# Rows of y by pure transposes, router logits by four column groups and a summing product: one change to a tuned attention-and-router kernel

## The chip, the cores and the metric

The kernel runs on one core of one Trainium2 chip. The metric is the device time in microseconds (us) of one execution of the whole program; the figure compared is the median over runs. Engines are named as the profile names them: PE is TensorE, PEld its weight loads, DVE VectorE, ACT ScalarE, POOL GpSimd, and SP the engine that issues most transfers.

## What the reference computes

A gated linear attention over 4 batches, 8 heads, 768 steps and 48 channels per head gives `y`. Its rows, seen as 3072 tokens of 384 channels, go through a router with two experts of eight per token. Cut to what matters here:

```python
for t in range(S):
    state = alpha[:, :, t, :, None] * state + np.einsum('bhd,bhe->bhde', k[:, :, t], v[:, :, t])
    y[:, :, t] = np.einsum('bhd,bhde->bhe', q[:, :, t], state)
x = np.ascontiguousarray(y.transpose(0, 2, 1, 3)).reshape(B * S, H * D)
logits = x @ w_gate
noise_scale = np.log1p(np.exp(x @ w_noise))
noisy_logits = logits + noise_scale * noise
top2 = np.argpartition(-noisy_logits, 2, axis=1)[:, :2]      # then a softmax over the two
h = np.maximum(x[mask] @ w1[e], 0.0)                          # for each expert e
out[mask] += top2_w[mask, k, None] * (h @ w2[e])
```

## The kernel before, in words

The tokens are cut into 24 **chunks** of 128 (six per batch). The attention runs chunk by chunk, with all eight heads as four pairs (`NP` = 4); a pair takes 128 partitions, 64 for each head, 48 of them used. The results of a chunk stand in `yT`, channels on partitions and tokens along the row.

The order of all work is written out by hand: every engine carries out its own queue in program order. The loop over `n` is one **chunk turn**. It emits pieces in the order of the string `ORDER`: among others `keys`, `alphas` and `queries` (four transposes each, L343, of the inputs of a later chunk), `turn_y` (rows of the chunk before, below), `turn_k` (four transposes of scaled keys, L450), `output` (products L491 and L252 into `y`, then the copy of `y` to `yT` on ACT, L494, or L487 in two halves at the start of a batch), `no_more` (an activation and the reading of its accumulator on ACT, L361), `state` (products L465), `scores` (products L423), `masked` (two masked copies on DVE, L443) and `products` (a scan on DVE, L371). `inverses` is the second scan on DVE, L383, to `over`. In the last chunk of a batch `state`, `turn_k` and `block` fall out of the turn that would prepare them, and in the first the product L491 does. A turn begins on PE with the eight transposes of `keys` and `alphas`.

`turn_y` is `rows_of`: for each pair one matrix product of `yT` with `to_rows` (L275), whose columns hold an identity that drops the unused channels, and beside it the router weights of the pair. One product so gives rows of y and a part of the logits, two pairs to a part. ACT copies the logits to `lgs` (L277), and the rows of y in two 16-bit planes to `y_sb` (L282), which SP writes to memory.

Routing of six chunks (`routing`, a generator) is cut into steps; `ROUTE` lists after which turn and place each step of the first two units comes (the turn is counted from the last chunk of the unit). The first steps are: the sum of the logits' parts on DVE (`lg`, L713) with an exponential on ACT (L719); a logarithm on ACT, ahead of which its table is loaded (L687); products with the noise (L728) and maxima on DVE; and then an exponential for the gates, again with a table load (L751). From turn 22 on, the pairs of expert tiles follow, ordered by due times in units of `T` = 20; `out_of_range` is one step among them.

Transfers, POOL's scaling of the keys (L401) and the PSUM pools (`h`: two buffers, used by `rows_of` and by products of the router) are unchanged in kind.

Of the kernel before, what the change touches and what calls it, by code (L numbers as in the profile page):

```python
# [12 lines left out]
U16 = mybir.dt.uint16  # L13
# [6 lines left out]
def kernel(  # L20
# [189 lines left out]
    to_rows = const.tile([C, NP, 2 * D + 2 * E], F32, name="to_rows")  # L210

    def place_ident():
        nc.gpsimd.memset(to_rows, 0.0)
        for i in range(2):
            for odd in range(2):
                nc.gpsimd.tensor_copy(
                    out=to_rows.rearrange("p (j o) c -> p j o c", o=2)[:, :, odd, ds(2 * E * odd + D * i, D)],
                    in_=ident[:, None, ds(DP * i, D)].to_broadcast([C, NP // 2, D]))

    def router_tile(on):  # L220
        w_r = on["one"].tile([C, NP, 2, E], F32, name="w_r")
        nc.gpsimd.memset(w_r, 0.0)
        return w_r

# [5 lines left out]
    def place_router(w_r):  # L230
        for odd in range(2):
            nc.gpsimd.tensor_copy(
                out=to_rows.rearrange("p (j o) c -> p j o c", o=2)[:, :, odd, ds((1 - odd) * 2 * D, 2 * E)],
                in_=w_r.rearrange("p (j o) w e -> p j o (w e)", o=2)[:, :, odd])

# [31 lines left out]
    def rows_of(n, yT, on):  # L267
# [24 lines left out]
    def fast_gla(on):  # L292
# [212 lines left out]

        ROUTE = (((1, 9), (2, 8), (2, 13), (3, 4), (3, 11), (4, 8), (4, 10), (5, 4), (5, 7)), ((1, 9), (1, 12), (2, 4), (2, 8), (2, 11), (3, 8), (3, 10), (4, 4), (4, 7), (4, 12)))
        routes = [routing(u, on) for u in range(NU)]
# [12 lines left out]
        def out_of_range(part):  # L520

            if part:
# [15 lines left out]
        return (load, load_v, alphas, no_more, products, inverses, keys, scaled_keys, queries, scores, masked, turn_k,  # L538
                state, block, output, turn_y, put_y, route, route_on, all_routed, out_of_range, places,
                clear_blocks, clear_yT)  # L540
# [559 lines left out]
    def pairs(on):  # L1100
# [11 lines left out]
        x_whole = x_turned.rearrange("p s w a t -> p s (w a t)").bitcast(F32)  # L1112
        xs = block([C, C], "xs", 5)
        hs = [block([C, FO // 2, C], f"h{f}", 2) for f in range(2)]
# [570 lines left out]
    with ExitStack() as es:  # L1685
        on = pools(es, "")
        shared = on["one"].tile([C, 2 * (NP * (C + 1) + 1) + 4 * NP * C], F32, name="shared")
        (load, load_v, alphas, no_more, products, inverses, keys, scaled_keys, queries, scores, masked, turn_k,
         state, block, output, turn_y, put_y, route, route_on, all_routed, out_of_range, places,
         clear_blocks, clear_yT) = fast_gla(on)  # L1690
# [4 lines left out]
        def beside():  # L1695

            at = (-0.95, 4.75, 3.66, 6.15, 6.9, 28.5)
            left = [(at[0], lambda: put_y(LAST - 2)), (at[1], lambda: output(LAST)), (at[2], lambda: turn_y(LAST - 1)),
                    (at[3], lambda: turn_y(LAST)), (at[4], lambda: put_y(LAST - 1)), (at[5], lambda: put_y(LAST)),
                    (5 * T + 17.4, lambda: out_of_range(0)), (5 * T + 18.7, lambda: out_of_range(1))]  # L1700
            r1, r2, r3 = (6.2, 12.2, 15.2)
# [21 lines left out]
        NOISE_AT = (3, 8, 13, 18)  # L1723
        FIRST_ORDER = "scores masked inverses keys router scaled turn_k queries alphas output products state turn_y"
        SECOND_ORDER = "keys turn_y inverses turn_k scaled queries no_more block output state alphas scores masked products"
        ORDER = "keys inverses alphas turn_y turn_k scaled queries block output no_more state scores masked products"

        LATE_ORDER = "keys inverses alphas turn_y turn_k scaled block output no_more state scores masked queries products"

# [12 lines left out]
        with tc.manual_schedule():  # L1742
# [3 lines left out]
            load(1, "kq")  # L1746
            place_ident()
            clear_blocks()
# [35 lines left out]
            for n in range(LAST):  # L1784
# [5 lines left out]
                          "state": lambda: state(n + 1), "scores": lambda: scores(n + 1),  # L1790
                          "masked": lambda: masked(n + 1)}
                names = (FIRST_ORDER if n == 0 else SECOND_ORDER if n == 1 else LATE_ORDER if n == LAST - 2 else ORDER).split()
                if n == 0:
                    pieces["router"] = lambda: place_router(held.pop(0))
# [73 lines left out]
```

## Time and profile before

| what | value |
|---|---|
| median of 3 runs | 629.37 us (628.87 to 629.84) |
| the profiled execution's own time | 634.14 us |
| its span on the core | 632.5 us |
| mean granted TensorE clock | 0.995 |
| busy PE, DVE, ACT, POOL | 613.7, 512.2, 330.4, 323.2 us |

The trace is of one execution, whose own time is 4.77 us above the median; what is worked out from it is a difference, to be laid on the median. Busy times are unions over the span. The chunk turns lie between about 20 and 153 us, the expert tiles behind.

### The profile page before, as it was taken

The numbers are of one execution on the slowest core, as the hardware profiler recorded it, in microseconds if no ns is written. First come the engines' busy times: TensorE is split into PE (matmuls) and PEld (weight loads), VectorE is DVE, ScalarE is ACT, GpSimd is POOL, SyncE is SP. The second block draws the span as 40 slices with busy tenths as digits, with TensorE's granted clock in tenths as the row PEclk, the third lists the DMA queues.
The fourth block names the chain that finished last, engine by engine and source line by source line (L and its number), as shares of the span: only waits on it lengthen the run. The fifth ranks groups of instructions, "written<-read, shape, count | busy, mean of one in ns | idle before, by whom it ended". The sixth has DMA issues, their size and how long they took to land.

```text
span 632.5 us, 14445 instructions
## 1 busy us (share of the span) xinstructions
PE 613.7 (97%) x5326; PEld 589.3 (93%) x5326; DVE 512.2 (81%) x1175; ACT 330.4 (52%) x664; POOL 323.2 (51%) x362
## 2 busy tenths in 40 slices
PE   8999999999999999999999999999999999999993
PEld 5899989988999999999999999999999999989893
DVE  8788998878759877578999999787987879878671
ACT  5778777675555453342555454545545545454340
POOL 7353277854051877775545465532655427443353
PEclk9999999999999999999999999999999999999997
DMA  9999999984862666785746776866869578775223
GB/s 144 167 199 214 219 201 170 226 160 112 264 194 100 205 199 182 205 248 98 176 103 134 176 242 135 225 149 154 260 161 234 123 181 226 178 213 134 63 40 53
DMA packets 178288, 108.56 MB, mean 172 GB/s; under 512 B 142600, under 2 KB 167667, under 8 KB 178209
## 3 DMA queue, kind: packets, MB, share of 16 engines
q1 hardware_dynamic: 137040, 33.59, 31.1%
q10 hardware_dynamic: 25840, 53.48, 27.7%
q0 software_dynamic: 15328, 20.47, 14.5%
q8 instruction: 44, 0.72, 0.5%
q14 instruction: 36, 0.29, 0.1%
HBM read 85.85 MB, written 24.22 MB: 174 GB/s over the span
## 4 chain that ended last, share of the span: by engine, by line
PE 75%; DVE 12%; issue 3%; DMA 3%; POOL 2%; ACT 2%; SPq 0%; POOLq 0%; DVEq 0%; ACTq 0%
PE h_ps L1338 14%; PE sc L1331 13%; PE o_ps L1338 11%; PE sc L1323 7%; PE c_ps L1331 6%; PE tp L343 5%; PE sc L423 4%; PE y L252 4%; PE h_ps L275 3%; PE y L491 3%; DVE wt L1204 1%; PE o_ps L465 1%; PE tp L450 1%; PE c_ps L1323 1%; DVE h L1207 1%
## 5 line engine op out<-in xcount | busy, mean ns | idle before, releaser
L972 POOL DMA_INDIRECT out_dram<-o,where x46 | 48.5, 1055 | 150.4 <-DVE o L1356 70.4
L1342 ACT ACTIVATE h<-h 128x512 f32<-128x512 f32 x89 | 55.2, 628 | 84.4 <-DVE h L1204 51.6
L988 POOL DMA_INDIRECT x_in<-x_rows,where x48 | 59.6, 1242 | 53.9 <-DVE where L1172 29.5
L980 POOL DMA_INDIRECT out_dram<-o,where x44 | 74.7, 1697 | 13.4 <-issue 13.4
L1338 PE MATMUL o_ps<-wt,hx 128*128 128x192 f32 x384 | 70.7, 327 | 0.0
L1338 PEld LDWEIGHTS o_ps<-wt,hx 128*128 128x128 f32 x384 | 61.5, 190 | 1.8 <-issue 1.8
L172 POOL DMA_INDIRECT table<-entry,place_u x48 | 53.1, 1106 | 13.9 <-issue 10.9
L1331 PE MATMUL sc<-yT,ws 128*128 128x128 f32 x408 | 56.5, 275 | 0.0
L1331 PEld LDWEIGHTS sc<-yT,ws 128*128 128x128 f32 x408 | 53.5, 191 | 0.0
L401 POOL TENSOR_TENSOR k_P<-k_P,over 128x512 f32<-128x512 f32 (+1 forms) x24 | 27.7, 1155 | 44.6 <-DVE over L383 31.5
L343 PE MATMUL tp<-ident,ins 128*128 128x128 f32 x288 | 42.0, 280 | 2.2 <-ACT k_P L393 0.7
L1352 ACT ACTIVATE o<-h_ps,tab 128x192 f32<-128x192 f32 x46 | 19.3, 420 | 40.9 <-PE h_ps L1338 33.7
L343 PEld LDWEIGHTS tp<-ident,ins 128*128 128x128 f32 x288 | 31.8, 142 | 7.2 <-ACT k_P L393 1.1
L443 DVE COPY_PREDICATED shared<-upto,sc 128x512 f32<-128x512 uint32 x47 | 31.9, 732 | 6.9 <-PE sc L423 6.4
L1338 PE MATMUL h_ps<-w,hx 128*128 128x192 f32 x192 | 35.6, 327 | 0.3 <-issue 0.3
L1338 PE MATMUL h_ps<-wt,h 128*128 128x192 f32 x192 | 35.3, 327 | 0.3 <-DVE wt L1204 0.3
L1338 PE MATMUL o_ps<-w,h 128*128 128x192 f32 x192 | 35.3, 327 | 0.2 <-DVE o L1360 0.2
L1338 PE MATMUL h_ps<-wt,hx 128*128 128x192 f32 x192 | 35.2, 326 | 0.0
L1338 PE MATMUL h_ps<-w,h 128*128 128x192 f32 x192 | 35.1, 326 | 0.0
L1198 ACT COPY xt<-x_turned 128x768 uint16<-128x768 uint16 x34 | 33.6, 1053 | 0.8 <-DMA x_turned<-x_in 0.8
L1338 PEld LDWEIGHTS h_ps<-w,hx 128*128 128x128 f32 x192 | 31.7, 190 | 0.7 <-issue 0.7
L1338 PEld LDWEIGHTS h_ps<-w,h 128*128 128x128 f32 x192 | 31.8, 190 | 0.0
(322 smaller groups left out, 1642.1 us busy)
## 6 DMA issues: line engine op xcount, KB each, us to landing
w<-in_moe_w_dram ACTq DMA_DIRECT2D x42, 512.0 KB
w<-in_moe_w_dram ACTq DMA_DIRECT2D x56, 384.0 KB
ins<-in_alpha_dram SPq DMA_DIRECT2D x24, 192.0 KB
ins<-in_k_dram SPq DMA_DIRECT2D x24, 192.0 KB
ins<-in_q_dram SPq DMA_DIRECT2D x24, 192.0 KB
vt<-in_v_dram SPq DMA_DIRECT2D x24, 192.0 KB
x_rows<-y_sb SPq DMA_DIRECT2D x24, 192.0 KB
ins<-in_moe_w_dram ACTq DMA_DIRECT2D x9, 512.0 KB
```

The lines of the kernel that those rows point to most:

```text
L172: put = nc.gpsimd.indirect_dma_start(out=table, out_offset=bass.IndirectOffsetOnAxis(ap=place, axis=0), in_=entry, in_offset=None, bounds_ ...
L343: nc.tensor.transpose(tp[:, j, :], src[:, 2 * j:2 * j + 2, :], ident)
L401: (nc.vector if n == NT - 1 else nc.gpsimd).tensor_tensor(c["k"][:, at], c["k"][:, at], over[:, at, 1:CB], op=ALU.mult)
L443: nc.vector.copy_predicated(MTs[n % 2][:, i], mask_upto, sc)
L972: put = nc.gpsimd.indirect_dma_start(out=out, out_offset=bass.IndirectOffsetOnAxis(ap=at, axis=0), in_=rows, in_offset=None, bounds_check= ...
L980: add = nc.gpsimd.indirect_dma_start(out=out, out_offset=bass.IndirectOffsetOnAxis(ap=at, axis=0), in_=rows, in_offset=None, bounds_check= ...
L988: nc.gpsimd.indirect_dma_start(out=rows, out_offset=None, in_=x_rows[0:units * UT, :], in_offset=bass.IndirectOffsetOnAxis(ap=at, axis=0), ...
L1198: nc.scalar.copy(halves[:, part], x_turned[:, :, part].rearrange("p s a t -> p s (a t)"))
L1323: nc.tensor.matmul(bank[name][:, f, :], W[:, ds(f * C, C)], X, start=new and f == 0, stop=True, skip_group_check=True)
L1331: nc.tensor.matmul(bank[name][:, 2 * h + f, :], W[h][:, ds(f * C, C)], X[h], start=new and not h and not f, stop=True, skip_group_check=True)
L1338: nc.tensor.matmul(bank[name], H[:, f, :], W[:, f, :], start=new and f == 0, stop=True, skip_group_check=True)
L1342: nc.scalar.activation(t, t if src is None else src, AF.Relu)
```

## The change

Rows of y are now made by four plain transposes of `yT` for chunks 0 to 21 (`turned_rows`); chunks 22 and 23 keep `rows_of`. The logits of those chunks are a separate piece, `logits`, behind `state`: four products with the router weights `w_r` (32 columns for each pair, 16 of them zero) as the stationary operand, one to each quarter of the output partitions; ACT copies the result to a spare tile `xs`. In the first piece of the next turn `sum_pairs` multiplies this copy with `two_parts` (ones that add two pairs), which turns it too, and ACT copies the 32 columns to `lgs`. The first routing steps come one turn later. `to_rows` is filled after turn 6 instead of at the start, and the second part of `out_of_range` is due later.

```diff
+    def turned_rows(n, yT, on):
+        bank = on["h"].tile([C, FO // 2, C], F32, name="h_ps")
+        for j in range(NP):
+            nc.tensor.transpose(bank[:, j, :], yT[:, j, :], ident)
+        y_sb = on["three"].tile([C, 2, NP, 2 * D], U16, name="y_sb")
+        planes = bank.rearrange("p j t -> p (j t)").bitcast(U16).rearrange("p (h c w) -> p w h c", h=H, w=2)
+        for w in range(2):
+            nc.scalar.copy(y_sb[:, w].rearrange("p j (i c) -> p (j i) c", i=2), planes[:, w, :, 0:D])
+        return y_sb
+
+    def logits_by_pair(yT, w_r, by_pair, on):
+        bank = on["h"].tile([C, FO // 2, C], F32, name="h_ps")
+        for j in range(NP):
+            nc.tensor.matmul(bank[ds(4 * E * j, 4 * E), 0, :], w_r[:, j].rearrange("p w e -> p (w e)"), yT[:, j, :], start=True, stop=True)
+        nc.scalar.copy(by_pair, bank[:, 0, :])
+        return bank, by_pair
+
+    def logits_by_token(n, bank, by_pair):
+        nc.tensor.matmul(bank[:, 1, 0:4 * E], by_pair, two_parts, start=True, stop=True)
+        nc.scalar.copy(lgs[(n // UC) % 2][:, n % UC].rearrange("p a c -> p (a c)"), bank[:, 1, 0:4 * E])
...
-                chunks[n]["y"] = rows_of(n, chunks[n]["yT"], on)
+                chunks[n]["y"] = (turned_rows if n < NT - 2 else rows_of)(n, chunks[n]["yT"], on)
...
-                    (5 * T + 17.4, lambda: out_of_range(0)), (5 * T + 18.7, lambda: out_of_range(1))]
+                    (5 * T + 17.4, lambda: out_of_range(0)), (6 * T + 7.0, lambda: out_of_range(1))]
...
-        ORDER = "keys inverses alphas turn_y turn_k scaled queries block output no_more state scores masked products"
+        ORDER = "keys inverses alphas turn_y turn_k scaled queries block output no_more state logits scores masked products"
...
-            place_ident()
...
-                pieces = [lambda: (load_v(n + 2), load(n + 5, "a" if n != 1 else ""), load(n + 4, "kq"), put_y(n - 2))] + \
+                pieces = [lambda: (load_v(n + 2), load(n + 5, "a" if n != 1 else ""), load(n + 4, "kq"), put_y(n - 2), sum_pairs(n - 2))] + \
...
+                if n == 6:
+                    last.append(lambda: (place_ident(), place_router(held[0])))
```

In `ROUTE` the first entries of the first unit go from `(1, 9), (2, 8)` to `(2, 6), (2, 8)`, and of the second from `(1, 9), (1, 12), (2, 4)` to `(2, 6), (2, 8), (2, 11)`.

PE's queue at the end of turn 7, in the kernel before: the products of the state, the scores of the next chunk (four pairs in two banks, written as eight rows of two kinds, of which two stand here), and the next turn's transposes.

```order
L252 MATMUL y<-shared,vt 48x128 x8
L465 MATMUL o_ps<-vt,k_end 64x48 x8
L423 MATMUL sc_1035<-q_P,k_P 128x128
L423 MATMUL sc_1036<-q_P,k_P 128x128
...
L343 MATMUL tp<-ident,ins 128x128 x8
L275 MATMUL h_ps<-to_rows,yT 128x112 x4
```

The same place of the changed kernel (its lines are numbered anew):

```order
L256 MATMUL y<-shared,vt 48x128 x8
L490 MATMUL o_ps<-vt,k_end 64x48 x8
L302 MATMUL h_ps<-yT,w_r 32x128 x4
L448 MATMUL sc_1084<-q_P,k_P 128x128
L448 MATMUL sc_1085<-q_P,k_P 128x128
...
L307 MATMUL h_ps<-two_parts,xs_169 128x32
L368 MATMUL tp<-ident,ins 128x128 x8
L292 MATMUL h_ps<-ident,yT 128x128 x4
```

The four narrow products stand ahead of the scores, and the summing product, which reads ACT's copy `xs`, ahead of everything in the next turn.

ACT's queue in turns 6 and 7 before, from the copies of `yT` at the start of the second batch on:

```order
L487 COPY yT<-y 48x512 x2
L719 ACTIVATE noisy<-lg 128x48
L361 ACTIVATE ins,above<-ins,less_150 128x8x48
L393 COPY k_P<-tp 128x512
...
L452 COPY k_end<-tp 128x512
L477 COPY S_block_157<-S_155 64x4x48 x2
L687 ACT_TABLE_LOAD
L687 ACTIVATE noisy<-noisy 128x48
L494 COPY yT<-y 128x512
L361 ACTIVATE ins,above<-ins,less_150 128x8x48
L393 COPY k_P<-tp 128x512
```

ACT's queue in turn 7 of the changed kernel:

```order
L477 COPY k_end<-tp 128x512
L752 ACTIVATE noisy<-lg 128x48
L502 COPY S_block_158<-S_156 64x4x48
L502 COPY S_block_158<-S_156 64x4x48
L720 ACT_TABLE_LOAD
L720 ACTIVATE noisy<-noisy 128x48
L519 COPY yT<-y 128x512
L386 ACTIVATE ins,above<-ins,less_151 128x8x48
L303 COPY xs_169<-h_ps 128x128
L308 COPY lgs_97<-h_ps 128x32
L418 COPY k_P<-tp 128x512
```

The exponential of the logits has moved from behind the copy of `yT` in turn 6 to ahead of the copies of `S_block` in turn 7, and the copy to `xs` stands behind all of it.

DVE's queue in turn 7 of the changed kernel, where the sum `lg` for that exponential stands:

```order
L468 COPY_PREDICATED shared<-upto,sc_974 128x512
L396 SCALAR_TENSOR_TENSOR P_all<-shared,least 128x516
L398 RECIPROCAL P_all<-P_all 128x4
L408 SCALAR_TENSOR_TENSOR over<-shared,P_all 128x515
L746 TENSOR_TENSOR lg<-lgs_96 128x96
L436 TENSOR_TENSOR q_P<-tp,P_all 128x512
```

Before, it stood behind `q_P` of turn 6; now it is behind the scan `over` of turn 7.

## Rows read from the trace of the kernel before

**Rows 1.** The page, busy time of each engine:

```profile
PE 613.7 (97%) x5326; PEld 589.3 (93%) x5326; DVE 512.2 (81%) x1175; ACT 330.4 (52%) x664; POOL 323.2 (51%) x362
```

**Rows 2.** The chain that ended last, turn 9: start, us, what:

```profile
67.74 1.02 PE tp L343 x8
68.76 0.88 PE h_ps L275 x8
69.64 0.44 PE tp L450 x4
...
70.51 0.89 PE y L491 x8
...
72.42 0.45 PE o_ps L465 x16
72.88 1.09 PE sc L423 x16
73.97 1.02 PE tp L343 x8
```

**Rows 3.** The chain, 405 to 420 us: four column groups:

```profile
411.59 1.43 PE h_half_ps L1643 x24
413.02 1.09 PE c_ps L1331 x8
```

**Rows 4.** The chain, 106 to 120 us: a small product ahead of a turn:

```profile
112.18 0.32 PE h_ps L831 x2
112.50 0.93 PE tp L343 x8
```

**Rows 5.** Timeline, ACT, end of turn 8: start, us, engine, line, operation, idle before:

```profile
66.24 0.59 ACT L494 COPY yT<-y 128x512 f32<-128x512 f32 x1 [0.76 <-PE y L252]
66.85 0.61 ACT L361 ACTIVATE ins<-ins,less 128x384 f32<-128x384 f32 x1
67.37 0.18 ACT L361 ACTIVATION_READ_ACCUMULATOR ins<-ins,less 128x1 f32 x1
68.36 0.59 ACT L393 COPY k_P<-tp 128x512 f32<-128x512 f32 x1 [0.80 <-PE tp L343]
```

**Rows 6.** Groups by form, ACT: copies from PSUM: busy us, mean ns:

```profile
L277 ACT COPY lgs<-h_ps 128x32 f32<-128x32 f32 x24 | 4.5, 188 | 8.0 <-PE h_ps L275 6.5 <-PE tp L450 0.7 <-issue 0.7
...
L356 ACT COPY shared<-tp 128x256 f32<-128x256 f32 x2 | 0.6, 376 | 2.2 <-PE tp L343 2.2
```

**Rows 7.** Timeline, ACT, turns 6 and 7:

```profile
53.91 1.17 ACT L487 COPY yT<-y 48x512 f32<-48x512 f32 x2
...
58.51 0.73 ACT L477 COPY S_block<-S 64x192 f32<-64x192 f32 x2
59.25 1.28 ACT L687 ACT_TABLE_LOAD   x1
60.55 0.24 ACT L687 ACTIVATE noisy<-noisy 128x48 f32<-128x48 f32 x1
60.70 0.57 ACT L494 COPY yT<-y 128x512 f32<-128x512 f32 x1
```

**Rows 8.** Timeline, DVE, turn 7:

```profile
58.25 1.23 DVE L383 TENSOR_TENSOR_SCAN over<-shared,P_all 128x515 f32<-128x515 f32 x1
```

**Rows 9.** The line of `lg`: duration in ns, least, median, most:

```profile
L713 DVE TENSOR_TENSOR lg<-lgs x4: 249/598/947, 54.4 to 202.5; 128x96 f32<-128x96 f32 x4
```

**Rows 10.** Timeline, ACT, turn 9:

```profile
73.58 0.23 ACT L751 ACTIVATE entry<-entry 128x12 f32<-128x12 f32 x1 [0.58 <-DVE entry L745]
...
74.69 0.19 ACT L361 ACTIVATION_READ_ACCUMULATOR ins<-ins,less 128x1 f32 x1
```

**Rows 11.** PE's waits over the whole span: us in total, times, longest:

```profile
PE tp L450 <- ACT noisy L687: 1.4, 1, 1.4
...
PE count L525 <- DVE out_of L536: 0.8, 1, 0.8
```

**Rows 12.** Timeline, POOL, at the start:

```profile
4.70 0.89 POOL L216 COPY to_rows<-ident 128x96 f32<-128x96 f32 x4
```

More of the change, by code (lines that the diff above doesn't have):

```diff
@@ L210 @@
     to_rows = const.tile([C, NP, 2 * D + 2 * E], F32, name="to_rows")
+    two_parts = const.tile([C, 4 * E], F32, name="two_parts")
     def place_ident():
@@ L220, in router_tile @@
     def router_tile(on):
-        w_r = on["one"].tile([C, NP, 2, E], F32, name="w_r")
+        w_r = on["one"].tile([C, NP, 4, E], F32, name="w_r")
         nc.gpsimd.memset(w_r, 0.0)
+        nc.gpsimd.tensor_tensor(two_parts.rearrange("p (h c) -> p h c", h=2),
+                                *(ident.rearrange("p (h o c) -> p h o c", h=2, o=2)[:, :, o, 0:2 * E] for o in range(2)), op=ALU.add)
         return w_r
@@ L233, in place_router @@
                 out=to_rows.rearrange("p (j o) c -> p j o c", o=2)[:, :, odd, ds((1 - odd) * 2 * D, 2 * E)],
-                in_=w_r.rearrange("p (j o) w e -> p j o (w e)", o=2)[:, :, odd])
+                in_=w_r[:, :, 0:2].rearrange("p (j o) w e -> p j o (w e)", o=2)[:, :, odd])
     def load_noise(u):
@@ L497, in turn_y, with logits, sum_pairs @@
             if 0 <= n < NT:
-                chunks[n]["y"] = rows_of(n, chunks[n]["yT"], on)
+                chunks[n]["y"] = (turned_rows if n < NT - 2 else rows_of)(n, chunks[n]["yT"], on)
+        def logits(n, w_r):
+            if n >= 0:
+                chunks[n]["logits"] = logits_by_pair(chunks[n]["yT"], w_r, on["spare"][n % 2], on)
+        def sum_pairs(n):
+            if n >= 0:
+                logits_by_token(n, *chunks[n].pop("logits"))
         def put_y(n):
@@ L502, in put_y @@
                 put_rows(n, chunks[n].pop("y"))
-        ROUTE = (((1, 9), (2, 8), (2, 13), (3, 4), (3, 11), (4, 8), (4, 10), (5, 4), (5, 7)), ((1, 9), (1, 12), (2, 4), (2, 8), (2, 11), (3, 8), (3, 10), (4, 4), (4, 7), (4, 12)))
+        ROUTE = (((2, 6), (2, 8), (2, 13), (3, 4), (3, 11), (4, 8), (4, 10), (5, 4), (5, 7)), ((2, 6), (2, 8), (2, 11), (2, 13), (3, 4), (3, 8), (3, 10), (4, 4), (4, 7), (4, 12)))
         routes = [routing(u, on) for u in range(NU)]
@@ L538, in fast_gla @@
         return (load, load_v, alphas, no_more, products, inverses, keys, scaled_keys, queries, scores, masked, turn_k,
-                state, block, output, turn_y, put_y, route, route_on, all_routed, out_of_range, places,
+                state, block, output, turn_y, logits, sum_pairs, put_y, route, route_on, all_routed, out_of_range, places,
                 clear_blocks, clear_yT)
@@ L1112, in pairs @@
         x_whole = x_turned.rearrange("p s w a t -> p s (w a t)").bitcast(F32)
-        xs = block([C, C], "xs", 5)
+        xs = on["spare"] = block([C, C], "xs", 5)
         hs = [block([C, FO // 2, C], f"h{f}", 2) for f in range(2)]
@@ L1688 @@
         (load, load_v, alphas, no_more, products, inverses, keys, scaled_keys, queries, scores, masked, turn_k,
-         state, block, output, turn_y, put_y, route, route_on, all_routed, out_of_range, places,
+         state, block, output, turn_y, logits, sum_pairs, put_y, route, route_on, all_routed, out_of_range, places,
          clear_blocks, clear_yT) = fast_gla(on)
@@ L1697, in beside @@
             at = (-0.95, 4.75, 3.66, 6.15, 6.9, 28.5)
-            left = [(at[0], lambda: put_y(LAST - 2)), (at[1], lambda: output(LAST)), (at[2], lambda: turn_y(LAST - 1)),
+            left = [(-1.1, lambda: sum_pairs(LAST - 2)), (at[0], lambda: put_y(LAST - 2)), (at[1], lambda: output(LAST)), (at[2], lambda: turn_y(LAST - 1)),
                     (at[3], lambda: turn_y(LAST)), (at[4], lambda: put_y(LAST - 1)), (at[5], lambda: put_y(LAST)),
-                    (5 * T + 17.4, lambda: out_of_range(0)), (5 * T + 18.7, lambda: out_of_range(1))]
+                    (5 * T + 17.4, lambda: out_of_range(0)), (6 * T + 7.0, lambda: out_of_range(1))]
             r1, r2, r3 = (6.2, 12.2, 15.2)
@@ L1723 @@
         NOISE_AT = (3, 8, 13, 18)
-        FIRST_ORDER = "scores masked inverses keys router scaled turn_k queries alphas output products state turn_y"
-        SECOND_ORDER = "keys turn_y inverses turn_k scaled queries no_more block output state alphas scores masked products"
-        ORDER = "keys inverses alphas turn_y turn_k scaled queries block output no_more state scores masked products"
-        LATE_ORDER = "keys inverses alphas turn_y turn_k scaled block output no_more state scores masked queries products"
+        FIRST_ORDER = "scores masked inverses keys scaled turn_k queries alphas output products state turn_y logits"
+        SECOND_ORDER = "keys turn_y inverses turn_k scaled queries no_more block output state logits alphas scores masked products"
+        ORDER = "keys inverses alphas turn_y turn_k scaled queries block output no_more state logits scores masked products"
+        LATE_ORDER = "keys inverses alphas turn_y turn_k scaled block output no_more state logits scores masked queries products"
         unread = []
@@ L1790 @@
                           "state": lambda: state(n + 1), "scores": lambda: scores(n + 1),
-                          "masked": lambda: masked(n + 1)}
+                          "masked": lambda: masked(n + 1), "logits": lambda: logits(n - 1, held[0])}
                 names = (FIRST_ORDER if n == 0 else SECOND_ORDER if n == 1 else LATE_ORDER if n == LAST - 2 else ORDER).split()
                 if n == 0:
-                    pieces["router"] = lambda: place_router(held.pop(0))
                     del pieces["block"], pieces["no_more"]
```

## The prediction

> **What bounds the kernel now.** I read the page's busy times first: PE is busy for 97% of the span [rows 1]. Busy alone doesn't bind, so I read the chain of waits next, in the chunk turns that the change touches. Through a whole turn it stays on PE, each group starting where the one before ends: turn 9 runs from 67.74 to 73.97, 6.23 us, all of it PE's own groups [rows 2]. An ordinary turn therefore costs what PE issues in it, and whatever PE is made to wait for is added to the end. Third came the timeline of ACT in these turns, since the change hangs PE on ACT. ACT waits for PE twice a turn: 0.76 us before the copy of `yT` and 0.80 before the next turn's copy of `k_P` [rows 5]. It has slack, but in two pieces, and the work between `y` and the turn's end stands in one queue.
>
> **PE's own groups.** Four float32 products stand in the trace as eight records, four transposes as four. `rows_of` costs 0.88 a turn, four transposes 0.44 [rows 2]: 0.44 saved.
>
> The four narrow products are eight records in two rounds of four. The nearest row has 24 records in four column groups with 256 columns: 1.43 us, 0.24 for a round of four [rows 3]. With 128 columns a round should be about half; I take 0.22 for both rounds. The change of the array's layout comes on top: after that stretch the next eight full-size records take 1.09 [rows 3], and eight of that size undisturbed 0.89 [rows 2], so 0.20 for one return. Here the products come between two groups that use parts of the array already, so part of it is paid today. I take 0.28, with bounds 0.22 and 0.42. The Trainium skill's rule against this change is in "TensorEngine Tiling (Array Packing)", Key Properties: changing the tiling mode drains TensorE, while groups within a mode overlap. The trace agrees: 1.09 against 0.89 behind four column groups, and 1.02 for the eight transposes behind `scores` against 2 x 0.44.
>
> For the summing product there is a row at the very same place, between `scores` and the eight transposes: a product of full width with 8 columns (L831). It takes 0.32, and the transposes then 0.93 instead of 1.02 [rows 4]: 0.23 net. With 32 columns it can hardly be less; I take 0.23, with 0.12 (two records at 0.06) if its loads hide. The same page, Instruction Overhead, says that a product of one column takes as long as one of 60 and puts the overhead at some 60 cycles; by that the two records would come to about 0.05, an estimate, and the 22 turns would be 4.0 us better than my sum. The row above, 0.23 for 8 columns, speaks against it here.
>
> Together -0.44 + 0.28 + 0.23 = +0.07 a turn, in 22 turns **+1.5 us** (bounds: 22 x -0.10 = -2.2, 22 x 0.21 = +4.6). The transposes' gain is spent on what follows them.
>
> **The new wait.** The summing product is the first thing of a turn on PE and needs `xs`, which ACT copies behind `yT` and `no_more`. Queued behind it are the transposes and then everything of the turn; nothing on PE passes it. So whenever ACT is late, PE now stops at the turn's start. Before, a late ACT had the 0.80 us of slack at `k_P`.
>
> *An ordinary turn.* In turn 8 the copy of `yT` starts at 66.24 and `no_more` ends at 67.37 + 0.18 = 67.55 [rows 5]. The copy to `xs` has 128 columns, between 0.188 for 32 and 0.376 for 256 [rows 6]: I take 0.28, so it ends at 67.83. The transposes there start at 67.74 today [rows 2]; with the narrow products ahead of `scores` the summing product is due 0.28 later, at 68.0 (what is saved on the rows of y moves both sides alike). It fits by 0.2 us: no cost. The other copies on ACT are the 188 ns that were there.
>
> *Ends and starts of batches.* In turns 4, 10 and 16 the products of the state, 0.45 [rows 2], are absent between `y` and the turn's end, so the slack of 0.2 becomes a wait of 0.3. In turns 6, 12 and 18 the copy of `yT` takes 1.17 [rows 7] instead of 0.59, so a wait of 0.4 to 0.5. Three of each: **+2.3 us** (0 to 3.5).
>
> *Turns 7 and 13: the logits' exponential and logarithm.* Before, ACT did the exponential a turn earlier. Now both stand in turn 7 ahead of `yT`, and the exponential waits for `lg`, which DVE does behind the scan `over`. That scan ends at 58.25 + 1.23 = 59.48 [rows 8], bound by DVE's own queue. `lg` takes 0.25 to 0.95 [rows 9]; the long ones ran beside POOL's scaling of keys, which here waits for the same scan and comes behind, so I take 0.25: ACT's exponential starts at 59.75. Then from start to start, with the durations of [rows 5, 7]: exponential 0.15, `S_block` 0.74, table 1.30, logarithm 0.15, `yT` 0.47, `no_more` 0.70, `xs` 0.28, in all 3.8: `xs` is there at 63.55. PE is due at 67.74 - 6.23 = 61.5 for turn 8's start, with -0.44 + 0.28 for the groups and 0.5 for turn 6's wait 61.85. PE stops for 1.7 us. In turn 13 the order is the same: **+3.4 us** for both (2.0 if half of ACT's chain overlaps better; 4.8 if `lg` takes 0.95).
>
> *Turns 9 and 14: the gates.* Their exponential waits for DVE's maxima and starts at 73.58; `yT` and `no_more` follow and end at 74.69 + 0.19 = 74.88 [rows 10], `xs` at 75.15. PE is due at 73.97 - 0.16 = 73.8 [rows 2], a wait of 1.3. Turn 14 has the same order; the stop of turn 13 lets DVE catch up, but two more maxima have moved into it, so 1.2. **+2.5 us** (1.0 to 3.2).
>
> **What goes.** PE waits 1.4 us at `turn_k` for the logarithm of the second unit, which stood at the end of turn 12 [rows 11]: it moves, and is counted anew above: **-1.4**. The second part of `out_of_range` stopped PE for 0.8 until DVE was ready [rows 11]; due 8 us later it finds its operand: **-0.8**. Filling `to_rows` (POOL) leaves the start, where the loads set the pace, and goes to turn 6's end, where POOL sits idle until `over`: nothing. Without that cover its copies alone would hold up the scaling of the keys by 0.89 [rows 12]. The last summing product falls where PE waits for the tokens' rows anyway: nothing. Behind the turns nothing is moved, and PE is the bound there too, so the sum reaches the end.
>
> **Sum.** 1.5 + 2.3 + 3.4 + 2.5 - 1.4 - 0.8 = +7.5 us. The profiled execution would go from 634.14 to 641.6; laid on the median, 629.37 + 7.5 = **636.9 us**.
>
> **Rivals.**
> - *The sum never waits: faster.* If ACT has `xs` ready in every turn, the waits fall away: 0 + (-2.2 to 1.5) - 2.2, so 625 to 628.7, say 627. It needs ACT to be some 1.7 us earlier in turns 7 and 13, that is, the exponential not held by the scan. For it: ACT has 1.56 us of idle time a turn, and rows of y come 0.44 earlier. Against it: the idle time lies behind the late place, and the scan's end doesn't hang on PE. It decides at new waits below 1 us in all. Chance 0.10.
> - *About as before.* The waits come at their lower bounds, 0 + 2.0 + 1.0, less the 2.2 that go, with the groups between -2.0 and 0.4: 628.1 to 630.6. Chance 0.10.
> - *Every turn waits.* The 0.2 us of slack rests on a copy that no row shows. Were the copy as long as the 0.59 of 512 columns, fourteen more turns would wait 0.1 each, and with the groups at +4.6 and the waits at their upper bounds the sum is 1.4 + 4.6 + 3.5 + 4.8 + 3.2 - 2.2 = 15.3: up to 644.7. Chance 0.06 for over 641.5.
> - *The forecast*, a few long stops of PE in named turns: 0.74, own range 631 to 641.5.
>
> **Numbers.** 636.9 is the forecast's. The range reaches down to 629, into "about as before", of which 0.03 stays below, and up to 641.5; with 0.10 and 0.06 outside, 0.19 is left out. A measurement here tells about 0.2%, 1.26 us, from no change. Faster 0.10, same 0.10, slower 0.80.
>
> **What would show it.** In the trace after: four transposes at 0.44 and narrow products at 0.22 to 0.42 in each turn; PE waiting for `xs` on ACT at the starts of turns 8 and 14 (1 to 2.5 us) and of 10 and 15 (about 1); waits of some tenths at the starts of turns 5, 7, 11, 13, 17, 19; no wait of PE at `turn_k` of 1.4 and none at the count. Wrong it would be if ACT's copy to `xs` in turn 7 ended before 62, or if turns without routing took well under 6.2 us.

## The result

| | us | |
|---|---|---|
| kernel before, same comparison | 629.42 | median of 4 runs (628.87 to 629.84) |
| changed kernel | 638.29 | median of 4 runs (637.82 to 638.88) |
| ratio | 1.0142 | 95% interval 1.0124 to 1.0159 |

The change costs 8.9 us; 7.5 was forecast, 636.9 against 638.3. Two of the experiments' comparisons ran on chips on which the kernel before takes 633.2 and 633.5 us instead of 629.4 to 629.7, so a time is compared below by its ratio to the kernel before in the same comparison; the profiled execution before (634.14) resembles the former, the one after (638.24) the latter.

PE is still busy for 97% of the span, 2.5 us longer than in [rows 1]. The page after, busy time of each engine:

```profile
span 636.6 us, 14757 instructions
...
PE 616.2 (97%) x5458; PEld 586.6 (92%) x5458; DVE 512.1 (80%) x1175; ACT 334.6 (53%) x686; POOL 324.5 (51%) x363
```

An ordinary turn is still all PE. The chain of the changed kernel in turns 2 and 3 (start, us, what), which answers to [rows 2]:

```profile
31.17 0.36 PE h_ps L302 x8
31.52 1.09 PE sc L448 x16
32.61 0.34 PE h_ps L307 x2
32.95 0.91 PE tp L368 x8
33.86 0.44 PE h_ps L292 x4
34.30 0.52 PE tp L475 x4
34.81 0.44 PE tp L368 x4
...
37.62 0.35 PE h_ps L302 x8
```

From one group of narrow products (L302) to the next it is 37.62 - 31.17 = 6.45 us, against 6.23 before: 0.22 a turn, where 0.07 was forecast. The transposes (L292) take the 0.44 foreseen, the narrow products 0.36 instead of 0.28, the summing product with the eight transposes behind it 0.34 + 0.91 instead of 1.02, as assumed. What nobody asked for is 0.08 at `turn_k` (L475), 0.52 instead of 0.44.

The waits of PE over the whole span (us in total, times, longest), which answer to [rows 11]:

```profile
PE h_ps L307 <- ACT xs L303: 4.5, 8, 1.4
...
PE h_ps L307 <- ACT ins L386: 0.9, 1, 0.9
...
PE h_ps L307 <- DMA vt<-in_v_dram: 0.4, 1, 0.4
```

The waits of 1.4 at `turn_k` and 0.8 at the count are gone, and the summing product (L307) waits ten times, 5.8 in all. These ten stand at the starts of turns 5, 7, 8, 10, 11, 13, 14, 15, 17 and 19, which are the ten turns that the prediction named, and no other. The stop put down to `ins` (`no_more`, just ahead of `xs` on ACT) is that of turn 14, the one put down to a DMA that of turn 13. Turns 8 and 14 (0.90 and 0.87) stay a little under the 1 to 2.5 us foreseen; turns 10 and 15 (0.66 and 1.38) lie to either side of the 1 us foreseen. Three of the four largest, from the timeline of PE (start, us, engine, line, operation, idle before):

```profile
64.74 0.41 PE L307 MATMUL h_ps<-two_parts,xs 128*128 128x32 f32 x2 [0.90 <-ACT xs L303]
...
78.38 0.41 PE L307 MATMUL h_ps<-two_parts,xs 128*128 128x32 f32 x2 [0.66 <-ACT xs L303]
...
112.38 0.41 PE L307 MATMUL h_ps<-two_parts,xs 128*128 128x32 f32 x2 [1.38 <-ACT xs L303]
```

Turn 7 on ACT, in the timeline, shows the forecast chain link by link (before: [rows 5, 7]):

```profile
61.06 0.24 ACT L752 ACTIVATE noisy<-lg 128x48 f32<-128x48 f32 x1 [0.48 <-DVE lg L746]
61.21 0.70 ACT L502 COPY S_block<-S 64x192 f32<-64x192 f32 x2
61.92 1.28 ACT L720 ACT_TABLE_LOAD   x1
63.22 0.24 ACT L720 ACTIVATE noisy<-noisy 128x48 f32<-128x48 f32 x1
63.37 0.57 ACT L519 COPY yT<-y 128x512 f32<-128x512 f32 x1
63.83 0.62 ACT L386 ACTIVATE ins<-ins,less 128x384 f32<-128x384 f32 x1
64.35 0.19 ACT L386 ACTIVATION_READ_ACCUMULATOR ins<-ins,less 128x1 f32 x1
64.44 0.25 ACT L303 COPY xs<-h_ps 128x128 f32<-128x128 f32 x1
```

And DVE there, which answers to [rows 8, 9]: `lg` is the short one, behind the scan. Ahead of the two scans stand the masked copies; before (first fence) DVE came to them without a wait, now (second fence) it waits for the scores at the end of turn 6:

```profile
55.54 1.35 DVE L443 COPY_PREDICATED shared<-upto,sc 128x512 f32<-128x512 uint32 x2
```

```profile
56.91 1.35 DVE L468 COPY_PREDICATED shared<-upto,sc 128x512 f32<-128x512 uint32 x2 [0.83 <-PE sc L448]
...
59.64 1.23 DVE L408 TENSOR_TENSOR_SCAN over<-shared,P_all 128x515 f32<-128x515 f32 x1
60.79 0.23 DVE L746 TENSOR_TENSOR lg<-lgs 128x96 f32<-128x96 f32 x1
```

From the exponential to the end of the copy to `xs` it is 64.69 - 61.06 = 3.6 us, 3.8 forecast. But the scan starts 1.4 later than before (59.64 against 58.25), because DVE waits 0.83 for the late scores of turn 6, and PE is due later still: the stop is 0.9, not 1.7. The prediction had the scan bound by DVE's own queue; in the changed kernel its time hangs on PE too.

### The profile page after: what moved, and what is told of

The parts are those of the page before. It is cut to its first block, busy times and chain, and to the rows that moved or that the text cites. A ratio compares the mean times of both kernels' runs of the same rounds, so it can differ in the third digit from the quotient of the medians.

```text
span 636.6 us, 14757 instructions
## 1 busy us (share of the span) xinstructions
PE 616.2 (97%) x5458; PEld 586.6 (92%) x5458; DVE 512.1 (80%) x1175; ACT 334.6 (53%) x686; POOL 324.5 (51%) x363
## 4 chain that ended last, share of the span: by engine, by line
PE 76%; DVE 13%; ACT 4%; issue 3%; DMA 2%; POOL 1%; SPq 0%; POOLq 0%; DVEq 0%; ACTq 0%
PE h_ps L1371 16%; PE sc L1364 14%; PE o_ps L1371 12%; PE sc L1356 8%; PE c_ps L1364 6%; PE tp L368 4%; PE y L256 3%; PE sc L448 2%; PE y L516 2%; PE c_ps L1356 1%; PE h_ps L292 1%; ACT ins L386 1%; DVE wt L1237 1%; DVE over L408 1%; PE tp L475 1%
## 5 line engine op out<-in xcount | busy, mean ns | idle before, releaser
L1494 ACT COPY m<-sc 128x512 f32<-128x512 f32 x17 | 10.0, 585 | 42.3 <-PE sc L1364 42.3
```

## The experiments

The steps of the routing behind the logarithm are called by these names: the *maxima* (DVE), the *gates* (the exponential on ACT), the *counts* (DVE), and the *rank*, two products of the counts that take a buffer of `h` (L819 and L820 in the changed kernel). The *count* is another product, that of `out_of_range`.

How many us a turn is longer than in the first profile of the kernel before is worked out from the timelines (from the start of one `scores` to the next), for the turns that tell the kernels apart; the last column but one adds all turns except 18:

| kernel | 3 | 5 | 7 | 8 | 10 | 13 | 14 | 15 | 18 | 19 | all but 18 | ratio |
|---|---|---|---|---|---|---|---|---|---|---|---|---|
| changed | .22 | .47 | .73 | 1.19 | .85 | -.83 | 1.16 | 1.85 | -1.73 | .90 | 8.85 | 1.0142 |
| sum late | .18 | .18 | .16 | .91 | 1.44 | -1.39 | .84 | 4.80 | -1.40 | .23 | 8.63 | 1.0095 |
| `lg` ahead of scan | .22 | .47 | .73 | .56 | .84 | -.74 | .56 | 1.88 | -.23 | 1.13 | 8.42 | 1.0103 |
| narrow twice | .44 | .47 | .73 | 1.42 | .85 | -.74 | 1.30 | 1.86 | .54 | 1.01 | 12.04 | 1.0226 |
| plain logits | .40 | .40 | .39 | .40 | .88 | -.35 | .40 | .85 | -1.60 | .40 | 8.21 | 1.0133 |
| sum and rank late | .18 | .18 | .16 | .93 | .27 | -1.39 | .85 | 2.75 | -1.77 | .23 | 5.39 | 1.0089 |
| routing behind `xs` | .22 | .46 | .73 | .52 | 1.03 | -.83 | .52 | 1.75 | -1.73 | .90 | 7.27 | 1.0126 |
| `no_more` behind `xs` | .22 | .22 | .21 | 1.12 | .23 | -1.34 | 1.10 | 2.14 | -.65 | .42 | 6.17 | 1.0086 |
| the same, `lg` ahead | .22 | .22 | .21 | .22 | .24 | -1.33 | .84 | 1.95 | -.61 | .42 | 5.49 | 1.0053 |
| before, two waits less | 0 | 0 | 0 | 0 | 0 | -1.55 | 0 | .81 | 0 | 0 | -.81 | 0.9982 |
| before, gates behind | 0 | 0 | 0 | 0 | 0 | -1.56 | 0 | 1.36 | -2.00 | .36 | .51 | 0.9998 |
| before, second unit like first | 0 | 0 | 0 | 0 | 0 | -1.55 | 0 | -.34 | -2.01 | 1.21 | -.46 | 0.9969 |

Turn 18 is 1.4 to 2.0 us shorter than in that first profile in seven of them, whatever the edit; run 9 takes this up. The changed kernel itself was timed only where the kernel before takes 629.4 us. Runs 1 to 4 and 9 to 12 stand beside 633.2 or 633.5, and a ratio there holds turn 18 and the stops among the experts too, which differ from profile to profile. So where a ratio and the turns tell different amounts, the turns are the nearer measure of what an edit did to them; each is from one execution.

My theory: the cost is PE's own groups plus stops of the summing product behind what ACT does ahead of `xs`. The rivals: the stops would come back elsewhere in any order; or the groups cost nothing.

### 1. The sum later in the turn

```diff
-..., put_y(n - 2), sum_pairs(n - 2))] + \
+..., put_y(n - 2))] + \
-"turn_k": lambda: turn_k(n + 1),
+"turn_k": lambda: (turn_k(n + 1), sum_pairs(n - 2)),
```

> The changed kernel with one edit: the summing product (with its copy to lgs) stands behind turn_k instead of at the turn's start; same work, other order. Theory: of the 8.9 us, PE's groups are some 4.8 (22 turns, 6.23 to 6.45 us each) and the waits of the summing product for xs some 6.0, less the 2.2 that went. Behind turn_k the product is due some 1.8 us later than at the start, more than the longest wait (1.4), so the waits go and the groups stay: 638.3 - 5.3 = 633.0 us, 631 to 635.4 (the transition behind the scores may come back at 0.1 a turn; the sum between two groups of full layout may cost less than 0.23). PE's waits at the sum are under 1 us in all. Rival 1, ACT is late in any order and the wait comes back at the copy of k_P: 636.5 or more, with as much PE waiting before turn_k. Rival 2, the groups cost nothing and all was the wait: 629 or less.

Measured: 639.42 beside 633.45, ratio 1.0095 (1.0076 to 1.0114), 3.0 us better than the changed kernel by the ratios instead of 5.3, and only 0.2 better by the turns (8.63 against 8.85). The stops at the sum are gone; turns 5, 7 and 19 fall to the bare price of the groups. But other stops are new. Of the two buffers of `h` the late sum still holds one, and the rank's products stand, in turns 10 and 15, until `y_sb` has been copied out of the other; in turn 8 a late copy of `k_P` is waited for instead. PE's waits, whole span:

```profile
PE h_ps L819 <- ACT y_sb L296: 2.9, 2, 1.8
...
PE tp L475 <- ACT k_P L418: 0.6, 1, 0.6
```

Behind the stop of 1.84 in turn 15 PE runs slower for 3 us. Timeline of PE, and then the window (PE, PEld, DVE, ACT, POOL busy, granted clock, DMA share, GB/s):

```profile
112.93 0.44 PE L819 MATMUL h_ps<-counts,before 128*128 128x48 f32 x2 [1.84 <-ACT y_sb L296]
...
114.54 1.09 PE L368 MATMUL tp<-ident,ins 128*128 128x128 f32 x4
115.43 1.74 PE L516 MATMUL y<-q_P,S_block 128*128 128x128 f32 x8
```

```profile
114.00:116.00 2.00, 2.00 (x12) 2.00 (x11) 1.91 (x4) 1.36 (x5) 1.19 (x2) 0.50 1.29 215
```

So the theory holds for the stops at the sum, and the edit made stops of its own, which run 6 takes up.

### 2. `lg` ahead of the scan

```diff
-        noisy, lg = noisy_logits(u, on)
+        lg = sum_logits(u, on)
+        if planned and u < 2:
+            yield
+        noisy = noisy_logits(u, on, lg)
...
-ROUTE = (((2, 6), (2, 8), ...), ((2, 6), (2, 8), ...))
+ROUTE = (((2, 1), (2, 6), (2, 8), ...), ((2, 1), (2, 6), (2, 8), ...))
```

> The changed kernel with one edit: in turns 7 and 13 DVE adds lg ahead of the scan over instead of behind it; the exponential keeps its place on ACT. Theory of the prediction, the exponential is held by the scan: ACT's 0.48 us of idle time ahead of it goes, xs comes 0.48 earlier, and PE's wait at the starts of turns 8 and 14 falls from about 0.94 to 0.45 each: 638.3 - 0.9 = 637.4, 636.8 to 637.9. Rival, the table load and what else stands in ACT's queue set the wait and the scan does not: 638.3, with the wait as before.

Measured: 640.17 beside 633.45, ratio 1.0103 (1.0082 to 1.0124). The whole time can't tell 0.9 us, but the turns can: turns 8 and 14 are 0.63 and 0.60 shorter (others are longer, turns 17 and 19 by 0.3 and 0.2; whether by the edit isn't shown). ACT's exponential no longer idles, and PE's stop goes from 0.90 to 0.27. Timeline, ACT and PE:

```profile
60.71 0.29 ACT L754 ACTIVATE noisy<-lg 128x48 f32<-128x48 f32 x1
...
64.41 0.41 PE L307 MATMUL h_ps<-two_parts,xs 128*128 128x32 f32 x2 [0.27 <-ACT xs L303]
```

The exponential was held by the scan.

### 3. The narrow products twice

```diff
-        for j in range(NP):
+        for j in (*range(NP), *range(NP)):
```

> The changed kernel with one edit: the four narrow products are issued twice in a row, to the same place, so the output is the same. Theory, a group of narrow products is two rounds of about 0.11 us, and the rest of its 0.36 is the change of the array's layout, paid once: 22 x 0.22 = 4.8 more, 643.1 us, 642.5 to 643.8. Rival, no price of the layout, the eight records take 0.36 wherever they are: 22 x 0.36 = 7.9 more, 646.2. The second four also delay the copy to xs and PE alike, so the waits stay.

Measured: 646.75 beside 633.45, ratio 1.0226 (1.0198 to 1.0254), 5.3 us over the changed kernel by the ratios (3.2 to 7.4 with both intervals), 3.2 by the turns. The chain shows the doubled group:

```profile
31.23 0.57 PE h_ps L302 x16
31.81 1.09 PE sc L448 x16
```

0.57 - 0.36 = 0.21 for the second four, and 0.22 in the turns without a stop (turn 3: .44 against .22). So two rounds cost the 0.22 that the prediction took, and some 0.14 comes once in a group, where it took 0.06. That this part is the change of layout is the reading of it; the run shows only that it isn't paid twice. The rival, 0.36 for the second four and 7.9 us, falls by the chain, and 7.9 lies outside that range. One part of the expectation failed: turns 5, 7, 10 and 15 are no longer than in the changed kernel, so a stop can shrink by what PE is given to do ahead of it.

### 4. The kernel before without its two waits

```diff
-((1, 9), (1, 12), (2, 4), (2, 8), (2, 11), (3, 8), (3, 10), ...
+((1, 9), (2, 8), (2, 11), (2, 13), (3, 4), (3, 8), (3, 10), ...
-(5 * T + 18.7, lambda: out_of_range(1))
+(6 * T + 7.0, lambda: out_of_range(1))
```

> The kernel before with the two edits of the change that have nothing to do with the logits: the count of out_of_range at 6 T + 7.0 and the second unit's logarithm in the turn after its exponential. Theory of the prediction: the waits of 1.4 at turn_k and 0.8 at the count go and nothing takes their place: 629.4 - 2.2 = 627.2, 626.6 to 628.0. Rival, the logarithm's table load only holds up another copy of that turn, and behind the count another product is late anyway: 629.4, within 0.5.

Measured: 632.63 beside 633.45, ratio 0.9982 (0.9969 to 0.9995): about half of the forecast gain. Turn 13 gains 1.55, turn 15 gives 0.81 back: the maxima came later, and the gates' exponential, ahead of `yT` on ACT, waits for them. Timeline, ACT and PE:

```profile
104.89 0.23 ACT L751 ACTIVATE entry<-entry 128x12 f32<-128x12 f32 x1 [1.73 <-DVE at_f L740]
...
105.64 0.59 PE L275 MATMUL h_ps<-to_rows,yT 128*128 128x112 f32 x3 [0.50 <-ACT yT L494]
```

The 0.8 at the count comes back too. PE waits for the count no more, but it waits 1.3 instead of 0.2 for DVE's `o` among the experts, some 20 us behind the count's old place. From the last `scores` to the end it is 479.9 us in both profiles. PE's waits behind the turns, in the kernel before and in this run:

```profile
PE o_ps L1338 <- DVE o L1360: 0.2, 1, 0.2
```

```profile
PE o_ps L1338 <- DVE o L1360: 1.3, 1, 1.3
```

So of the two gains only the one at `turn_k` reached the end in this execution, and half of it was given back: the rival has the count right.

### 5. Plain logits

```diff
+        for j in range(NP):
+            nc.tensor.matmul(logits[:, 0, ds((j // 2) * 2 * E, 2 * E)], yT[:, j, :], w_r[:, j].rearrange("p w e -> p (w e)"),
+                             start=j % 2 == 0, stop=j % 2 == 1)
```

> The kernel before with rows of y by four pure transposes and the logits by four products of full width with 16 columns each (eight records, in a bank of their own, behind the transposes): no narrow products, no xs, no summing product, the routing where it was. It prices a record of few columns. Theory, from rows of this case: a record of 128 x 128 weights takes 0.08 to 0.12 us however few its columns (rank's four records with 48 columns 0.44, the sum's two with 32 columns 0.23), so the eight take 0.7 to 0.9 and a turn 0.44 + 0.8 - 0.88 = 0.3 to 0.45 more: 22 times, 7 to 10 us slower, ratio 1.011 to 1.016. Rival, such a product costs only as much as its few columns (0.02 to 0.04 a record): -0.44 + 0.24 a turn, 4.4 us faster, ratio 0.993.

Measured: 638.07 beside 629.71, ratio 1.0133 (1.0118 to 1.0149), as the theory had it. The chain: eight records with 16 columns each take 0.80, 0.10 a record.

```profile
33.97 0.44 PE h_ps L288 x4
34.40 0.80 PE h_ps L290 x8
35.20 0.48 PE tp L464 x4
```

Few columns make a product with 128 x 128 weights hardly cheaper than 112 did (0.88). The narrow products with the sum, for all their layout, are the cheaper of the two ways: 0.22 a turn against 0.40.

### 6. Sum and rank late

Run 1, and in the two lists of `ROUTE`:

```diff
-(4, 10), (5, 4), (5, 7)
+(4, 10), (5, 9), (5, 11)
...
-(3, 10), (4, 4), (4, 7), (4, 12)
+(3, 10), (4, 9), (4, 11), (4, 12)
```

> The run with the late sum again, with one more edit: the rank's products, which stopped there for 1.1 and 1.8 us until y_sb was copied out of the bank that they take next, stand behind the turn's output. Theory: these two waits, and the 1.5 us of halved clock behind the second, were made by that edit alone and go; what is left over the kernel before is the price of PE's groups, 22 x 0.18 = 4.0, less 1.4 and 0.8, plus 0.6 at turn_k and 0.5 at turn_y: +2.9 us, ratio 1.0046, 1.003 to 1.0065. Rival, the bank is missing wherever the rank stands, so it waits there: ratio 1.008 or more.

Measured: 635.12 beside 629.71, ratio 1.0089 (1.0076 to 1.0103). The rank no longer waits for `y_sb` and the clock doesn't fall, but 2.5 us over the expectation stay. Turn 8 keeps 0.75 and turn 15 is 2.75 longer: the exponentials still hold up ACT, and now the copies of `k_P` and `yT` come too late. PE's waits:

```profile
PE tp L475 <- ACT k_P L418: 1.9, 3, 0.7
...
PE h_ps L292 <- ACT yT L519: 0.5, 1, 0.5
PE h_ps L864 <- DVE picked L825: 0.4, 1, 0.4
```

The late sum with the late rank buys 3.3 us (3.5 by the turns); where ACT itself is held by DVE, the stop goes to the next reader. The rival's ratio came true, but not by its mechanism, since the rank no longer waits for its buffer.

### 7. The kernel before, gates behind `no_more`

On top of run 4:

```diff
-(3, 4), (3, 8), (3, 10), (4, 4)
+(3, 4), (3, 10), (3, 12), (4, 4)
```

> The kernel before with the two waits less, as in the earlier run, and the second unit's gates behind no_more instead of ahead of the copy of yT, where they stopped PE for 0.5 (turn 15 became 0.8 longer). Theory: this 0.8 goes too, so turn 13's 1.55 is kept whole, and with the count's 0.8 the time is 2.3 us under the kernel before: ratio 0.9964, 0.995 to 0.998. Rival, the table load of 1.28 ahead of the gates now holds up the copy of k_P, and PE stops at turn_k instead: ratio 0.998 to 1.0.

Measured: 629.65 beside 629.71, ratio 0.9998 (0.9989 to 1.0007). Neither theory nor rival in its mechanism: `turn_k` doesn't wait, the rank does. PE's waits:

```profile
PE h_ps L786 <- DVE counts L774: 1.0, 1, 1.0
```

The chain maxima, gates, counts, rank was shortened at its front and not at its end. Turns 19 and 20 are 0.36 and 0.57 longer besides, with stops of PE at `turn_k` for POOL's scaling of the keys (0.14 and 0.35); whether they come from the edit isn't shown.

### 8. Logarithms and gates behind `xs`

```diff
-((2, 6), (2, 8), (2, 13), (3, 4), (3, 11), (4, 8), (4, 10), (5, 4), (5, 7))
+((2, 6), (2, 12), (2, 15), (3, 4), (3, 11), (4, 12), (4, 14), (5, 7), (5, 9))
-((2, 6), (2, 8), (2, 11), (2, 13), (3, 4), (3, 8), (3, 10), (4, 4), (4, 7), (4, 12))
+((2, 6), (2, 12), (2, 15), (3, 3), (3, 5), (3, 12), (3, 14), (4, 7), (4, 9), (4, 12))
```

> The changed kernel with the logarithms and the gates of both units behind the copy to xs instead of ahead of yT; the rank two steps later. Theory, what stands ahead of xs on ACT is what the sum waits for: the four waits of turns 7, 9, 13 and 14 (0.94, 0.63, 0.94, 1.6, in all some 4.2) go from the sum; the table load and the step, 1.43, now stand ahead of k_P, which has slack, and cost PE some 0.3 each at turn_k. 3 us less than the changed kernel, ratio 1.0095, 1.008 to 1.0115. Rival, the stop only moves to turn_k with its whole length, as the 1.4 of the kernel before: ratio 1.013 or more.

Measured: 637.34, ratio 1.0126 (1.0110 to 1.0141): 1.0 better than the changed kernel by the ratios, whose intervals overlap, and 1.6 by the turns, where 3 was forecast; the time leaves it open. The turns show two answers. Behind the logarithms (8 and 14) the stop falls by 0.65, as expected. Behind the gates (10 and 15) the sum waits no more, but the turns are no shorter, since counts and rank come late. Timeline of PE in turn 15:

```profile
109.67 0.41 PE L307 MATMUL h_ps<-two_parts,xs 128*128 128x32 f32 x2
...
111.59 0.63 PE L475 MATMUL tp<-ident,k_P 128*128 128x128 f32 x4 [0.18 <-ACT k_P L418]
...
112.91 0.44 PE L819 MATMUL h_ps<-counts,before 128*128 128x48 f32 x2 [0.25 <-DVE counts L807]
```

### 9. The kernel before again

> The kernel before, unchanged, for a second profile of it. Its first profiled execution took 634.14 us, 4.7 above the median; seven runs since have turn 18 some 2 us shorter than it or have it alike, and the run with plain logits, whose count stands where it stood before, shows no wait at the count. Theory: the 0.8 at the count, the 1.1 at L465 in turn 18 and some 1.4 among the experts belong to that one execution, so a profile near the median has turns 17 and 18 about 2 us shorter and no wait of 0.8 at the count: span 627 to 629. Rival, they are part of every execution and the 4.7 came from elsewhere: both waits are there again.

Measured: 634.49, where the kernel before has a median of 633.16, and a span of 632.9. The rival holds: both waits are there, and every turn is the first profile's within 0.04 us. PE's waits:

```profile
PE o_ps L465 <- ACT k_end L452: 1.1, 1, 1.1
PE count L525 <- DVE out_of L536: 0.8, 1, 0.8
```

So they belong to executions of the kernel before near 634. Whether one near 629.4 has them no profile of the unchanged kernel shows. In run 5, where the count stands as before and the kernel before takes 629.7, PE's waits don't have the 0.8. In run 10, in the same comparison as this run and with the count unmoved, they don't have it either, but PE waits 0.9 for DVE's `o` instead. And in run 4, which moves the count, the 0.8 comes back at `o`. So no trace shows a gain from moving the count; for the kernel before near 629.4 that is argued from these three.

### 10. The second unit's routing placed as the first's

```diff
-((1, 9), (1, 12), (2, 4), (2, 8), (2, 11), (3, 8), (3, 10), (4, 4), (4, 7), (4, 12))
+((1, 9), (2, 8), (2, 13), (3, 4), (3, 11), (4, 8), (4, 10), (5, 4), (5, 7), (5, 12))
```

> The kernel before with one edit: the second unit's routing steps take the same places as the first's, so its logarithm leaves the end of turn 12 and its maxima, gates and rank come half a turn to a turn later. The first unit's turns show no wait. Theory: the 1.4 to 1.55 at turn_k goes, and since gates and rank move along no chain of the routing gets shorter, so nothing takes its place: 1.5 us under the kernel before, ratio 0.9976, 0.9965 to 0.9988. Rival, as in the run with the gates behind no_more, the gain of turn 13 is given back at the rank or the gates: ratio 0.999 to 1.001.

Measured: 631.46 beside 633.16, ratio 0.9969 (0.9957 to 0.9982). Turn 13 gains 1.55, nothing comes back at gates or rank (turn 15 is 0.34 shorter, turn 16 0.20 longer, since the rank's own products move from one to the other). Turn 18 is 2.01 shorter and turn 19 1.21 longer, with two stops of some 0.25 in it; which part of this is the edit's isn't shown. By the ratio this version beats both kernels.

### 11. `no_more` behind the copy to `xs`

In `ORDER`, and alike in `LATE_ORDER`, the order of one late turn:

```diff
-"... block output no_more state logits scores masked products"
+"... block output state logits no_more scores masked products"
```

> The changed kernel with one edit: on ACT the copy to xs stands ahead of no_more (0.70) instead of behind it, in turns 2 to 22. Theory, the sum waits for what stands ahead of xs on ACT: xs comes up to 0.70 earlier in every late turn, so each stop at the turn's start loses up to 0.70: of about 0.2, 0.2, 0.2, 0.5, 0.5, 0.97, 0.94, 0.63, 1.4 and 0.7 there stay 0.3, 0.2 and 0.7. 4 to 4.5 us less than the changed kernel: ratio 1.0073, 1.0055 to 1.009. Rival, ACT's queue as a whole is late and the 0.70 stops PE at turn_k by way of the copy of k_P instead: ratio 1.0125 or more.

Measured: 639.22 beside 633.16, ratio 1.0086 (1.0065 to 1.0106), 3.5 us better than the changed kernel by the ratios, 2.7 by the turns. Turns 5, 7 and 10 lose their stops whole. Turns 8 and 14 keep nearly all of theirs, against the expectation: turn 7 now starts 0.9 us earlier, but the exponential, behind the scan, only 0.4 (60.66 against 61.06), so ACT just idles longer ahead of it. The scan follows the scores at the end of turn 6, and these, ahead of turn 7's stop, are only 0.4 earlier (55.31 against 55.71). In turn 15 a stop of 1.3 stays for the gates, where 0.7 was expected. Timeline, ACT and PE:

```profile
60.66 0.24 ACT L752 ACTIVATE noisy<-lg 128x48 f32<-128x48 f32 x1 [1.01 <-DVE lg L746]
...
63.75 0.41 PE L307 MATMUL h_ps<-two_parts,xs 128*128 128x32 f32 x2 [0.83 <-ACT xs L303]
```

### 12. Both: `no_more` behind, `lg` ahead

> The last edit (no_more behind xs) and the earlier one (lg ahead of the scan over) together in the changed kernel. Theory: the stops of turns 7 and 13 are then gone whole, another 0.5 in all, and what is left over the kernel before is the price of PE's groups, 21 x 0.22 = 4.6, a stop of some 0.7 for the gates of turn 14 and some tenths, less the 1.4 that went at turn_k: +4.0 us, ratio 1.0063, 1.0045 to 1.008. Rival, the groups' price is itself partly the wait and goes with it: ratio 1.003 or less.

Measured: 636.91 beside 633.16, ratio 1.0053 (1.0034 to 1.0072); the turns are 3.4 us shorter in all than the changed kernel's. Turn 8 stands at 0.22, PE's groups and nothing else. At the sum 1.1 stays for the gates of turn 14 and 0.6 at the start of turn 14; another 1.0 has come up at the state's products, which wait for `k_end` (in turns 12 and 18). PE's waits:

```profile
PE h_ps L307 <- ACT xs L303: 1.7, 2, 1.1
...
PE o_ps L490 <- ACT k_end L477: 1.0, 2, 0.6
```

The groups' price didn't go with the waits, so the rival falls.

## Why the prediction was right, and where its terms were not

| term | forecast | measured | from |
|---|---|---|---|
| PE's groups | +1.5 (-2.2 to 4.6) | +4.3 | turns 1 to 22, without 18, less their stops (where there is one, the turn's length in runs 11 and 12), added |
| ends and starts of batches | +2.3 | +2.0 | .25, .52, .24, .51, 0 and .48 at the starts of turns 5, 7, 11, 13, 17, 19 |
| turns 7 and 13 | +3.4 (2.0 to 4.8) | +1.9 | 1.19 - 0.22 and 1.16 - 0.22 |
| gates | +2.5 | +2.2 | 0.85 - 0.24 and 1.85 - 0.22 |
| wait at `turn_k` | -1.4 | -1.55 | turn 13 of run 10 |
| count | -0.8 | most likely 0 | runs 4, 5, 9 and 10 |
| sum | +7.5 | +8.9 | the medians too differ by 8.9 |

Turn 17 counts as 0 because it is no longer than in runs 11 and 12, though the trace shows a stop of 0.18 there. Turn 18 is left out because its length before differs between executions; against the 5.34 us that it takes in runs 7 and 10 the groups would come to 0.3 more.

The mechanism was right: the summing product stops PE at the starts of the ten named turns and no other, and runs 1, 2, 11 and 12 take most of these stops away along the named chains; those of turns 14 and 15 they only shorten or trade for others. Three sizes were off: the groups by +2.8, turns 7 and 13 by -1.5, the count by +0.8. Since the second error hides half of the first, that the sum came within 1.4 us is in part luck.

*PE's own groups* is the term that failed most, almost at its upper bound. Two of its parts: what was put down to the change of layout costs 0.14 in a turn, not 0.06 (run 3), so "part of it is paid today" held for less than assumed; and 0.08 at `turn_k` was not on the list. The summing product at 0.23 came out as taken. By the Trainium skill, "TensorEngine Tiling (Array Packing)", Instruction Overhead, its two records would have come to some 0.05, an estimate; the trace and run 5 don't agree with that. A rule that comes nearer is on another page of the Trainium skill, "TensorE: Matmul & The Clock Gate", LDWEIGHTS (loading the stationary operand): a weight load takes a time set by its columns, by its formula 107 ns for 128, an estimate. Run 5's 0.10 a record agrees; that the load is what sets it was not tried apart.

*Turns 7 and 13* came out under the lower bound. The chain on ACT was right, 3.6 of 3.8. The error is in when PE is due: one turn's groups and one stop were added up to there, 0.34 in all, while seven turns' groups (1.5) and the stops at turns 5 and 7 (0.25 and 0.52) had moved PE by 2.3 us, against a scan that moved by 1.4. Nor was the scan bound by DVE's own queue alone: DVE waits 0.83 for turn 6's scores, so it is late with PE, but without the stop at turn 7's start. The later PE comes, the smaller its next stop; run 11 is the same in reverse.

*The count* was a wait of a profiled execution 4.7 us above the median, taken whole as part of every execution (run 9 shows it again at 634.49); and where it does stand, taking it away only brought out a stop for DVE's `o` behind it (run 4).

Of the rivals, "the sum never waits" falls on both its legs: run 12, with less than a third of the waits at the sum, is still slower than the kernel before, and the groups alone cost more than what went. "About as before" falls with the waits, which took 6.1 us where it had 3.0. "Every turn waits" falls too: the copy to `xs` takes 0.25, the 0.28 assumed, and turns 2, 3, 6 and 9 don't wait.

## What to carry to other kernels

Before a product is put at the head of the bounding engine's queue, look what its operand stands behind on the engine that makes it, and put it as late in that queue, and its operand's copy as early, as the buffers allow: moving `no_more` alone was worth 2.7 of the 8.9 us in the turns (run 11). When a step of a chain is moved (maxima, gates, counts, rank), the last reader's place has to move too, or the wait only changes its name. A wait that only an execution above the median shows should enter a sum with a chance, not whole, and before any wait is counted as a gain, look how late the next operand of the same engine is.

## What the hardware showed that I had not expected

- Behind stops of PE of 0.49 and 1.84, between 109.9 and 112.9 us (run 1), the granted clock was 0.50 in the stretch from 114 to 116 us, 1.2 instead of 2.4 GHz, and four transposes took 0.89 from start to start instead of 0.44. A single stop of 1.38 in the changed kernel was followed by no such stretch: its eight transposes took the usual 0.91.
- A product of 128 x 128 weights with 16 columns took 0.10 us a record (run 5), hardly less than one with 112 columns (0.88 for eight).
- The four transposes of `turn_k` took 0.52 us directly behind the four of the rows of y, 0.48 behind products with 16 columns (run 5) and 0.44 behind products with 112 (before); why was not tried.
